# Building the first FFT's filter by casting loads instead of permutation matmuls, with stage A in four parts and products from ScalarE copies

## The chip, the cores and the metric

One core of one Trainium2 chip. The metric is the device time of one execution in microseconds (us). Most figures are medians of three to eleven executions. Each execution has a state, and all compared here are of the fast state (the single execution of before_look can't be given one). The rounds of experiments ran on different chips, so each ratio is against the kernel before in the same round. Traces are of one execution each. A trace's span is about 2 us less than the time of the same execution.

Engines are named as in the profile: PE is TensorE (PEld its weight loads), DVE is VectorE, ACT is ScalarE, POOL is GpSimd, SP is SyncE. "Granted clock" is the TensorE clock that was let through, 1.00 being full speed.

## The reference

```python
# batch 8, seq 3008, dim 256; then 24064 tokens, 256 -> 2048 -> 256
X = np.fft.rfft(x, axis=1)
F = (filt_r + 1j * filt_i)[None, :, :]
y = np.fft.irfft(X * F, n=x.shape[1], axis=1)
x = y.reshape(B * S, D)
h = np.maximum(x @ w_in, 0.0)
return (h * h @ w_out).astype(np.float32)
```

The FFT is made of matmuls with f16 constants. For one batch the stages are: A (x to u, written to DRAM and read back turned), B (u to the spectrum), products with the filter, P (products to ze), Z written to DRAM (dZ) and read back turned (zt), Y (zt to yt, the input of the feed-forward). For batch 0, stage A's result is turned on the chip and not through DRAM. Feed-forward then runs in 47 groups of 512 tokens, eight slots each, with the FFT stages of later batches laid into the slots.

## The kernel before

These are the parts that the change touches. The filter comes as float32 in dense rows; 0/1 matrices on PE put it in the order that the products need (psf), and ACT evicts it with the sign of the imaginary part:

```python
def place_f(im, k, *engs, rotate=False):
    ...
            nc.tensor.matmul(o, sPF[:, PQ.index((0, q)), :], f16s[0][:, im, a:a + d1 - d0],
                             start=True, stop=False)
            q, a = divmod(e1 + d0, QF) if c else (0, QF + d0)
            nc.tensor.matmul(o, sPF[:, PQ.index((1, q)), :], f16s[0][:, im, a:a + d1 - d0],
                             start=False, stop=True)
    ...
        if eng is nc.scalar:
            eng.activation(out=dst, in_=src, func=AF.Copy, scale=sign[:, 0:1] if im else 1.0)
```

Products are taken by DVE straight from PSUM; x of batch 1 and the weights come as float32 on SyncE's queue and are cast on the chip:

```python
    nc.vector.tensor_mul(
        out=prod,
        in0=ps.rearrange("p (a d) -> p a d", d=D).unsqueeze(1).to_broadcast([128, 2, 2, D]),
        in1=sF[:, :, 2 * p:2 * p + 2, :])

def load_wout(k):
    if k == 0:
        w32s[2] = p_h2.tile([128, NJT, 256], F32, tag="h2", name="wout32")
    c = slice(8 * k, 8 * k + 8)
    nc.sync.dma_start(out=w32s[2][:, c, :],
                      in_=moe_w_out.rearrange("(jt r) c -> r jt c", r=128)[:, c, :])
```

The prologue, cut to its order. While batch 0's Z travels through DRAM, 12 of the 16 units of batch 1's stage A are computed:

```python
for k in range(3):
    cast_wide(0, k, nc.vector, nc.gpsimd if k == 2 else nc.vector)
...                                  # constants, w_in, x of batch 1 (three loads of 1 MB)
for c in (0, 2, 1, 3):
    chunk_a0(c)                      # stage A of batch 0
...                                  # turn_u, first place_f
for k in range(7):
    if k < 6:
        unit_b(0, 2 * k)
        if k < 5:
            place_f(1, k + 1, nc.scalar)
        unit_b(0, 2 * k + 1)
    if k > 0:
        unit_p0(k - 1)
    if k < 4:
        place_f(0, k + 2, nc.scalar)
...
read_z(0, 0)
load_wout(0)
read_z(0, 1)
load_wout(1)
for c in (0, 2, 1):
    chunk_a(1, c)                    # stage A of batch 1, 12 of 16 units
for c in (0, 2, 1):
    write_u(1, c)
```

## Time and profile before

| | before |
|---|---|
| time, median of 3 (range) | 763.81 us (763.39 to 764.84) |
| span of the traced execution (time 765.42 us) | 763.6 us |
| stage A of batch 0 ends (last uT) | 17.75 us |
| last product of batch 0 ends | 40.55 us |
| first matmul of stage Y | 48.48 us |
| first feed-forward matmul (psH) | 49.93 us |
| first output matmul (psO) | 62.16 us |

The prediction below shows the main lines. Two more views are used later. First the DMA queues of the kernel before (packets, bytes, and the time that their packets took as a share of all 16 engines' span; q1 carries the loads of SyncE and ScalarE, q0 those of GpSimd):

```profile
q1 hardware_dynamic: 85704, 87.38, 37.1%
q0 software_dynamic: 19008, 20.43, 20.3%
```

q1 moved 87.38 MB in 0.371 x 763.6 = 283 us of full engine time, or 308 GB/s; q0 20.43 MB in 155 us, or 132 GB/s. The megabytes need care: a load that casts is counted by the f16 that it writes, and it reads twice that. The list of DMA issues shows it for w_out, here in the kernel before (float32) and in the changed kernel (cast), with the KB of each issue:

```profile
wout<-in_moe_w_out_dram SPq DMA_DIRECT2D x2, 1024.0 KB
...
sWout<-in_moe_w_out_dram POOLq DMA_DIRECT2D x2, 512.0 KB, 13.1
```

Of q0's bytes 9.4 MB are such loads of x (9184 KB in the list), the rest are the accumulating transfers of the products. Counted as read, q0 moved 29.8 MB, or 192 GB/s: a byte took 1.6 times as long as on q1, not more than twice.

Then two stretches of the busy time by stretch (length, then PE, weight load, DVE, ACT, POOL with their instructions, granted clock, DMA share, GB/s):

```profile
60.00:70.00 10.00, 9.29 (x65) 6.06 (x65) 7.16 (x10) 6.30 (x10) 0.00 (x0) 1.00 0.31 83
...
120.00:140.00 20.00, 19.91 (x246) 14.65 (x244) 17.36 (x21) 15.63 (x25) 0.00 (x0) 1.00 0.78 217
```

In the first group (60 to 70 us) DVE has room and the DMA engines are mostly idle; from 120 us on PE is saturated.

### The profile page before, as it was taken

To read this page: it belongs to the slowest core of one execution; us is meant where nothing else is said; L and a number is where in the kernel's file an instruction comes from. 1 tells how busy PE (TensorE), PEld (TensorE's weight loads), DVE (VectorE), ACT (ScalarE), POOL (GpSimd) and SP (SyncE) were. 2 spreads that over 40 slices of the span, in tenths; PEclk is the share of its full clock that TensorE was granted. 3 is DMA by queue.
4 is the path that set the end of the run, shared out by engine and by line. 5 is a ranking of instruction groups with operands and counts; after the bars stand their busy time and mean duration, and the time that the engine had idled before them with its cause. 6 is when DMAs were issued, how large, how long until landed. Compare 5 with 4: busy or idle time off the path is not lost.

```text
span 763.6 us, 19701 instructions
## 1 busy us (share of the span) xinstructions
PE 749.8 (98%) x8262; PEld 552.9 (72%) x8262; DVE 645.8 (85%) x714; ACT 578.8 (76%) x841; POOL 192.4 (25%) x260
## 2 busy tenths in 40 slices
PE   8988999999999999999999999999999999999998
PEld 5845766777777777877778777787777777777776
DVE  5857998899889888988979898798989989888783
ACT  3966777888877887788877877877877777777773
POOL 3800750244222321222312324033311222000000
PEclk9999999999999999999999999999999999999999
DMA  9985798765786467745585656775447334321011
GB/s 364 391 229 182 115 173 214 208 115 117 154 218 133 89 123 172 191 102 125 115 211 123 120 120 115 201 147 109 101 122 198 89 72 99 98 76 50 29 57 57
DMA packets 104946, 109.26 MB, mean 143 GB/s; under 512 B 9640, under 2 KB 93096, under 8 KB 102936
## 3 DMA queue, kind: packets, MB, share of 16 engines
q1 hardware_dynamic: 85704, 87.38, 37.1%
q0 software_dynamic: 19008, 20.43, 20.3%
q8 instruction: 65, 1.06, 0.6%
q14 instruction: 25, 0.20, 0.1%
q10 hardware_dynamic: 144, 0.18, 0.1%
HBM read 58.12 MB, written 48.23 MB: 139 GB/s over the span
## 4 chain that ended last, share of the span: by engine, by line
PE 88%; DVE 6%; DMA 3%; ACT 1%; issue 1%; POOL 0%; SPq 0%; ACTq 0%; DVEq 0%
PE psH L553 39%; PE psX L666 20%; PE psY L666 14%; PE psB L442 3%; PE psY L523 2%; PE psA L358 2%; PE psP L487 2%; DVE h L564 2%; PE psO L573 2%; DVE prod L450 1%; DMA ut<-dU 1%; PE warm L272 1%; DMA dU<-u 1%; PE psf L291 1%; PE psf L294 1%
## 5 line engine op out<-in xcount | busy, mean ns | idle before, releaser
L557 ACT ACTIVATE h<-psH 128x1024 f16<-128x1024 f32 x376 | 384.6, 1024 | 151.6 <-PE psH L553 147.4
L553 PE MATMUL psH<-yt,sWin 128*128 128x512 f16 (+7 forms) x1728 | 388.3, 352 | 1.4 <-DVE yt L532 0.6
L564 DVE TENSOR_TENSOR h<-h 128x2048 f16<-128x2048 f16 (+1 forms) x192 | 229.8, 1197 | 48.3 <-ACT h L557 48.0
L457 POOL DMA_DIRECT2D prod<-prod x168 | 138.6, 965 | 438.0 <-DVE prod L450 429.1
L553 PEld LDWEIGHTS <-sWin 128*128 128x128 f16 x1728 | 152.2, 98 | 99.4 <-issue 4.8
L666 PEld LDWEIGHTS <-sum 128*128 128x128 f16 x2880 | 177.5, 98 | 20.2 <-issue 0.2
L666 PEld LDWEIGHTS <-h 128*128 128x128 f16 x2160 | 133.6, 98 | 21.0
L450 DVE TENSOR_TENSOR prod<-psB,sF 128x1024 f16<-128x1024 f32 x84 | 102.4, 1219 | 16.4 <-PE psB L442 16.2
L666 PE MATMUL psX<-sT,sum 128*128 128x128 f16 x1440 | 102.5, 219 | 0.0
L666 PE MATMUL psY<-sT,sum 128*128 128x128 f16 x720 | 69.7, 219 | 0.0
L642 DVE TENSOR_TENSOR sum<-sum,h 128x2048 f16<-128x2048 f16 x45 | 55.0, 1222 | 1.0
L666 PE MATMUL psY<-sWout,h 128*128 128x128 f16 x720 | 55.0, 219 | 0.0
L666 PE MATMUL psX<-sT,h 128*128 128x128 f16 x720 | 54.9, 219 | 0.0
L666 PE MATMUL psY<-sWout,sum 128*128 128x128 f16 x720 | 54.7, 219 | 0.1
L645 DVE TENSOR_TENSOR sum<-h 128x2048 f16<-128x2048 f16 x45 | 54.8, 1217 | 0.0
L648 DVE TENSOR_TENSOR sum<-h,sum 128x2048 f16<-128x2048 f16 x45 | 54.7, 1217 | 0.0
L639 DVE TENSOR_TENSOR sum<-h 128x2048 f16<-128x2048 f16 x45 | 54.7, 1215 | 0.0
L362 ACT CAST u<-psA 96x512 f16<-96x512 f32 x90 | 52.2, 580 | 3.2 <-PE psA L358 2.8
L532 DVE CAST yt<-psY 128x376 f16<-128x376 f32 x62 | 33.7, 544 | 20.0 <-PE psY L523 19.9
L489 ACT CAST ze<-psP 128x512 f16<-128x512 f32 x84 | 48.9, 584 | 0.6 <-PE psP L487 0.4
L666 PE MATMUL psX<-sWout,h 128*128 128x128 f16 x720 | 47.6, 219 | 0.0
L523 PEld LDWEIGHTS <-zt 112*128 112x128 f16 x512 | 33.5, 98 | 18.5 <-issue 4.3
(86 smaller groups left out, 644.4 us busy)
## 6 DMA issues: line engine op xcount, KB each, us to landing
zt<-dZ SPq DMA_DIRECT2D x64, 192.0 KB
dU<-u SPq DMA_DIRECT2D x28, 384.0 KB
prod<-prod POOLq DMA_DIRECT2D x168, 64.0 KB, 2.7
dZ<-ze SPq DMA_DIRECT2D x28, 384.0 KB
x<-in_x_dram POOLq DMA_DIRECT2D x40, 192.0 KB, 5.0
ut<-dU SPq DMA_DIRECT2D x7, 1024.0 KB
xw<-in_x_dram SPq DMA_DIRECT2D x6, 1024.0 KB
out_dram<-top SPq DMA_DIRECT2D x31, 128.0 KB
```

The lines of the kernel that those rows point to most:

```text
L362: nc.scalar.copy(out=o, in_=pv)
L450: nc.vector.tensor_mul(out=prod, in0=ps.rearrange("p (a d) -> p a d", d=D).unsqueeze(1).to_broadcast([128, 2, 2, D]), in1=sF[:, :, 2 * p:2 ...
L457: nc.gpsimd.dma_start(out=prod[64 * i:64 * i + 64, 0], in_=prod[64 - 64 * i:128 - 64 * i, 1], accum_op=mybir.AluOpType.add)
L489: nc.scalar.copy(out=zes[(b, c)][:, 2 * i6:2 * i6 + 2, :], in_=ps.rearrange("p (a d) -> p a d", d=D))
L553: nc.tensor.matmul(ps[:, i, o:o + n], sWin[:, dt, jt * 128:(jt + 1) * 128], yts[b][:, dt, r:r + n], start=(dt == 0), stop=(dt == 1))
L557: nc.scalar.activation(out=h2[:, 2 * s:2 * s + 2, :], in_=ps, func=AF.Relu)
L564: nc.vector.tensor_mul(out=v, in0=v, in1=v)
L639: nc.vector.tensor_add(out=t, in0=a21, in1=a22)
L642: nc.vector.tensor_sub(out=t, in0=f[5], in1=a11)
L645: nc.vector.tensor_sub(out=t, in0=a11, in1=a21)
L648: nc.vector.tensor_sub(out=t, in0=a12, in1=f[6])
L666: nc.tensor.matmul(o[:, t, :], f[p][:, q, 128 * t:128 * t + 128], sg["w"][p][:, q, :], start=(m == 0 and p in (1, 2)), stop=(q == 7), skip ...
```

## The change

The intent was to shorten the prologue: no permutation matmuls and no evictions for the filter. GpSimd loads the filter with a cast to f16 into half rows (real parts on 64 partitions, imaginary on the other 64); a DVE copy swaps the halves (turn_f); signs are set later (settle_f). ACT copies stage B's result to f16 in SBUF so that the product runs from 16-bit SBUF operands. Stage A is split into four parts. Also, w_in, w_out and batch 1's x become casting loads of GpSimd, and all of batch 1's stage A moves from the wait for Z into the first feed-forward groups; idle matmuls, fill(22), take its place. The core of the diff:

```diff
-    def place_f(im, k, *engs, rotate=False):
-    ...
+    def load_f(c0, c1):
+        for im, filt in enumerate((filt_r, filt_i)):
+            v = filt[0:1504, :].rearrange("(j c) d -> j c d", c=47)
+            a, p = max(c0, 1), 64 * im
+            nc.gpsimd.dma_start(out=sF[p:p + 32, 0, c0:c1, :], in_=v[:, c0:c1, :])
+            nc.gpsimd.dma_start(out=sF[p + 32:p + 64, 0, a:c1, :], in_=v[:, 47 - a:47 - c1:-1, :])
+    ...
+    def turn_f(c0, c1):
+        for i in (0, 64):
+            nc.vector.tensor_copy(out=sF[i:i + 64, 1, c0:c1, :],
+                                  in_=sF[64 - i:128 - i, 0, c0:c1, :])
+    def settle_f(c0, c1):
+        nc.vector.tensor_scalar_mul(out=sF[64:128, 1, c0:c1, :], in0=sF[64:128, 0, c0:c1, :],
+                                    scalar1=-1.0)
+        nc.vector.tensor_copy(out=sF[64:128, 0, c0:c1, :], in_=sF[0:64, 0, c0:c1, :])
     ... (load_wout, cut)
-        nc.sync.dma_start(out=w32s[2][:, c, :],
+        nc.gpsimd.dma_start(out=sWout[:, c, :],
+    FC = ((0, 6), (6, 12), (12, 18), (18, 24))
+    HALVES = ((0, 0), (1, 0), (0, 1), (1, 1), (2, 0), (2, 1))
     ... (unit_b)
+        if b == 0:
+            ub = p_prod.tile([128, 2, D], F16, tag="prod", name=f"ub_{p}")
+            nc.scalar.copy(out=ub, in_=pv)
+            pv = ub
     ... (fft_plan)
-                for a in range(12, 16):
-                    fixed.append((2 + a / 2, unit_a, b, a))
-                moves.append((10.5, read_u, b))
+                for a in range(16):
+                    fixed.append(((3 if a < 8 else 4) + a / 2, unit_a, b, a))
+                for q in range(8):
+                    moves.append((1 + q, settle_f, 3 * q, 3 * q + 3))
+                moves.append((12.5, read_u, b))
-                r = 13.5 + 15 * p / 11 if b == 1 else ...
+                r = 16.5 + 13.5 * p / 11 if b == 1 else ...
     ... (prologue)
-    for c in (0, 2, 1, 3):
-        chunk_a0(c)
+    for n, cs in enumerate(((0, 2), (0, 2), (1, 3), (1, 3))):
+        for h in HALVES[n + 2:n + 3] if n > 1 else HALVES[2 * n:2 * n + 2]:
+            cast_wide(*h)
+        chunk_a0(n % 2, *cs)
     ...
-    for c in (0, 2, 1):
-        chunk_a(1, c)
+    load_rest()                      # rest of batch 1's x, and w_out, once Z has landed
+    fill(22)
```

## The prediction

> **What bounds the kernel now.** I read the page's busy line first, then the busy time by stretch, then the chain of waits up to the first feed-forward matmul, then the timeline of ScalarE (ACT), VectorE (DVE) and the DMA queues in that stretch. The page's first lines and the busy time by stretch:
>
> ```profile
> span 763.6 us, 19701 instructions
> PE 749.8 (98%) x8262; PEld 552.9 (72%) x8262; DVE 645.8 (85%) x714; ACT 578.8 (76%) x841; POOL 192.4 (25%) x260
> ...
> 20.00:30.00 10.00, 9.89 (x106) 8.71 (x104) 9.54 (x12) 9.46 (x11) 7.79 (x13) 1.00 1.05 411
> 30.00:40.00 10.00, 9.42 (x87) 7.88 (x85) 8.06 (x8) 9.21 (x10) 8.89 (x12) 1.00 0.82 308
> 40.00:50.00 10.00, 7.44 (x54) 4.60 (x53) 5.74 (x8) 6.10 (x10) 0.00 (x0) 0.98 0.74 213
> 50.00:60.00 10.00, 9.70 (x48) 4.26 (x48) 4.91 (x7) 7.47 (x10) 0.00 (x0) 0.85 1.09 305
> ...
> 200.00:400.00 200.00, 199.69 (x2249) 148.27 (x2248) 172.89 (x187) 160.20 (x238) 50.67 (x69) 1.00 0.65 149
> ```
>
> The columns of a stretch are its length and then PE, weight load, DVE, ACT, GpSimd (POOL), the granted clock, the DMA share and GB/s. After the start PE has no slack: 199.69 of 200 us. There a change counts by the PE work it adds or removes. The change keeps that part almost untouched; it rebuilds the prologue, in which batch 0 is transformed before any feed-forward matmul can start. What releases that start is in the chain of waits:
>
> ```profile
> 36.94 0.87 PE psP L473 x8
> 37.81 0.23 PE psB L442 x2
> 38.08 0.11 DVE prods L450
> 38.20 2.36 DVE prods L450 x2
> 40.60 0.61 PE psP L473 x4
> 41.24 1.02 ACT ze L475
> 42.27 2.35 DMA dZ<-ze
> 44.76 3.58 DMA zt<-dZ
> 48.34 0.14 issue
> ...
> 49.40 0.48 ACT yt L530
> 49.93 2.29 PE psH L553 x5
> ```
>
> Read it backwards. Feed-forward begins at 49.93. The last product of batch 0 ends at 40.56, so a tail of 9.4 us (last inverse matmuls, copy, write to DRAM, read back, first stage Y) is fixed. The question is when the last product ends. Before it, ACT is the bound: 9.46 and 9.21 of 10 us in 20 to 40, in strict turns of filter eviction (sF, real and imaginary) and ze:
>
> ```profile
> 28.99 1.02 ACT L302 ACTIVATE sF<-psf 128x1024 f16<-128x1024 f32 x1
> 30.09 1.11 ACT L302 ACTIVATE sF<-psf,sign 128x1024 f16<-128x1024 f32 x1
> 31.18 1.01 ACT L475 CAST ze<-psP 128x1024 f16<-128x1024 f32 x1
> ```
>
> DVE is second, with products at 1.22 us each. The start of the input DMA sets the rest: one MB of x lands each 2.5 us (casts at 6.20, 8.71, 11.21), so the queue delivers about 420 GB/s, and it is full until about 36 us.
>
> **What the Trainium skill says.** (1) "VectorE: DVE Perf Modes", section "The perf-mode tier table": a tensor-tensor operation runs at twice the rate with 16-bit operands in SBUF and at single rate with any PSUM operand; a 16-bit copy reaches four times. The trace agrees for the first: the product from PSUM of 1024 elements takes 1.22 us, a 1024-element f16 subtraction (sT) 0.68. No f16 copy on DVE is in this trace. (2) "DMA: Bandwidth & Descriptors", section "Issuing engines are not separate DMA queues": all queues share the same 16 engines. The trace agrees so far as one queue alone shows a share of 1.05 at 411 GB/s: a second queue has no spare capacity to find. (3) "SBUF — State Buffer", section "Who interferes with whom": two-port DVE modes shut out GpSimd's descriptor generation. Not shown in this trace. (4) "TensorE: Matmul & The Clock Gate", part 1: half the clock after an idle window of some 3.4 us. The trace agrees: 512-column matmuls are 0.43 us apart at the start and again from 49.93 (12 matmuls in 4.26 us, granted clock 0.85), 0.21 when warm.
>
> **The change, part by part.**
>
> Removed from the path up to the last product: the 108 permutation matmuls (PE is not the bound there); 13 sF evictions on ACT (6.6 + 5.1 + 1.1 = 12.8 us); one f cast on ACT (1.0) and one on DVE (0.7); GpSimd's casts. DMA is also lighter: 3 MB of x for batch 1 no longer come first.
>
> Products: 12 x (1.22 - 0.68) = 6.5 us less on DVE, for 12 ACT copies of 128x512 at 0.58 = 7.0 us. New on DVE: eight half-row copies (turn_f, 64 x 1536 f16). From (1), by the page's form (1536/4 + 150 cycles at 0.96 GHz), I estimate 0.56 us each, 4.4 us together.
>
> So after stage A the two engines have, worked out:
> ACT: 7 turned evictions x 0.60 + 12 copies x 0.58 + 5 ze x 1.02 + one half ze 0.58 = 4.2 + 7.0 + 5.1 + 0.6 = 16.9 us.
> DVE: 5 evictions x 0.68 + 12 products x 0.68 + turn_f 4.4 + half ze 0.7 = 3.4 + 8.2 + 4.4 + 0.7 = 16.7 us.
> They are balanced and coupled (each product waits for its ACT copy), so I allow 1 to 1.5 us of bubbles: 18 us.
>
> Where stage A ends. Half loads of 0.5 MB should land at 5.1, 6.3, 7.6, ... 11.3 us at 420 GB/s. But GpSimd begins the filter loads when the second half has landed, and they then take up to half of the engines. About 1.2 MB of x remain at 7.5 us; at 210 to 250 GB/s they end, with one us of completion, at 13.3 to 14.3. Cast 0.7, last 32 matmuls 1.4, eviction 0.6: last uT at about 16.2 (before: 17.75). So splitting stage A wins only 1.5 us. First turned matmuls 0.4, then 18 us: last product (and half ze) near 34.5. The tail is then about 9.0 (9.4 less 0.4 for the split ze): **feed-forward starts near 43, 7 us earlier.**
>
> The filter loads: 16 DMAs with cast, and two rows. A first x load from GpSimd in the steady part is issued in 0.51 us, one behind others in 1.15, and lands 5.0 us (median, 4.2 to 7.7) after issue. Four per chunk: last chunk issued between 16 and 26 us, landed by 22 to 31. It is needed at about 29, three units before the end. So it is just hidden in my reckoning.
>
> After the start. Added: stage A of batch 1 wholly inside the feed-forward, 16 single 512-column matmuls instead of 8: +8 x 0.215 = +1.7 us of PE; 6 more ACT copies (0.57) and 6 more DVE copies (0.69); settle_f, 16 f16 operations of 64 x 768 estimated at 0.36 (same form), 5.7 us of DVE, against 2.7 us of w_out casts removed. In slots 3 to 7 DVE then has about 0.6 (square) + 0.7 (settle) + 0.7 (stage A) + 0.3 (yt) = 2.3 us a slot, more than PE's 1.5. That makes the first group about 13 us, against 12.2 before. Saved: 22 filler matmuls keep the clock, so the 12 slow matmuls go at 0.21: -2.6 us. In the chain, batch 1's u goes out to DRAM and back and PE stands until it lands:
>
> ```profile
> 67.03 3.21 DMA dU<-u
> 70.26 3.83 DMA ut<-dU
> 74.14 0.39 PE psB L442 x2
> ```
>
> The wait counted for PE there is 1.3 us. The change puts the first stage-B unit five slots (some 10 us) after the last stage A, before it was three to four; the round trip is 7.1, so this wait should go: -1.3. Against it, 12 products are squeezed into 13.5 slots in place of 15, while DVE was busy all of 81.22 to 110.80 (14.38 of 14.38 and 15.08 of 15.20 us): I add 1 us. Sum after the start: +1.7 + 0.8 - 2.6 - 1.3 + 1 = -0.4, with the doubt on the plus side of DVE; some of the 2.6 was hidden behind ACT. I take -1 to +1, centre -0.5.
>
> **Total:** 763.8 - 7 - 0.5, rounded to **756 us**, 1.0% faster.
>
> **The rivals.**
> (a) The filter DMA becomes the bound: reversed rows are 192 pieces of 1 KB per DMA and GpSimd generates every one; DVE's casts and f16 copies may shut it out. For it: 16 issues at 1.15 us with landings up to 7.7 us, on engines that are already full. Against: 3 MB of x and the GpSimd casts are gone, and 0.51 us issues exist. The last chunk landing at 36 in place of 30 would bring the start to 48: about 761.
> (b) The early groups turn DVE-bound, or w_out and the second half of x for batch 1 come too late, since both wait for Z to land and go through GpSimd one after the other (w_out in 1 KB rows). For it: 2.3 us a slot against 1.5, and w_out is needed only about 13 us after the start. Each would cost 2 to 5 us: 758 to 761.
> (c) PE falls to the half clock in the prologue itself: it loses 108 matmuls and has only about 10 us of work in 18. Then 8-matmul steps take 1.7 us, fills 9.4 and the tail grows: 2 to 4 us back, 759.
> (d) Everything overlaps better than the old schedule: the last product at 30, the tail at 8.5, two more us from the removed waits. Start at 38.5: 750 to 751. To pass 2% (748.5) the start would have to come near 36, which balanced sums of 16.9 and 16.7 us after a stage A that ends at 16 do not allow, unless stage A ends by 14 with no bubbles.
> (e) The transfer is hidden anyway, and nothing moves: not likely, because the permutation's evictions stand on the chain (6.5% of the first 52 us as ACT sF alone, and 21.6% as PE psf).
>
> **Range and chances.** Start at 43 give or take 4, after-part give or take 2.5: 748.5 to 761.5, eight times in ten. Faster by over 2% needs (d) and more: 0.10. Slower by over 2% needs 779, a stall of over 20 us in a part where the old trace has none of that kind: 0.02. Within 2%: 0.88.
>
> **What would show it.** Right: last product near 34, first feed-forward matmul near 43; ACT and DVE both about nine tenths busy from 17 to 34; products in 0.68; no slow 512-column matmuls at the start; the stretch from 100 us after the start on is the same as before. Wrong in stage A: the second half of x lands well after 13.3 to 14.3. Wrong in (a): DVE waits for DMA before turn_f. Wrong in (b): PE idle before psO or psA with a DMA as releaser, or evictions of DVE as releaser in the first two groups. Wrong in (c): granted clock below 0.9 between 15 and 40. The prediction fails altogether if the tail of 9 us changes, since I took it over, or if the DMA rate of the filter loads is half of what I took.

## The result, and the profile after

The changed kernel took **773.54 us** (median of 4, 772.38 to 778.20) against 764.33 (763.39 to 765.91) for the kernel before on the same chip. The ratio is 1.013, with a 95% interval of 1.008 to 1.018. A ratio here is the mean time of one kernel's fast runs over that of the other's of the same rounds, so not quite the ratio of the medians. That is within 2%, but slower, and 12 us above the top of the predicted range. The traced execution is the slowest of the four (778.20 us; the others took 772.38 to 774.55), so its lags below are on the high side.

The first two lines of the page of the changed kernel:

```profile
span 776.2 us, 19474 instructions
PE 747.3 (96%) x8148; PEld 548.7 (71%) x8148; DVE 646.4 (83%) x734; ACT 572.0 (74%) x843; POOL 188.7 (24%) x262
```

PE is 2.5 us less busy over a span 12.6 us longer: the loss is waiting, not work. The busy time by stretch says where:

```profile
10.00:20.00 10.00, 5.05 (x71) 4.57 (x72) 5.48 (x10) 1.88 (x5) 6.27 (x11) 0.74 1.10 337
20.00:30.00 10.00, 7.66 (x73) 6.50 (x71) 6.22 (x11) 5.99 (x12) 5.41 (x11) 0.67 1.07 168
...
60.00:70.00 10.00, 6.98 (x44) 3.67 (x43) 9.58 (x18) 5.93 (x9) 0.00 (x0) 1.00 0.93 183
...
120.00:140.00 20.00, 17.41 (x172) 11.92 (x169) 14.30 (x17) 13.78 (x23) 3.02 (x6) 0.94 0.90 214
```

Against the rows of before, three places stand out. From 10 to 30 us no engine is near full and the granted clock is 0.74 and 0.67. From 60 to 70 us DVE is full (9.58) and PE is not. From 120 to 140 us PE loses 2.5 us and the clock falls again. And the DMA engines are full (1.07 in 20 to 30) at 168 GB/s, where before the same stretch moved 411 GB/s at 1.05 (part of this gap is the counting of casting loads). The queues of the whole run:

```profile
q1 hardware_dynamic: 82408, 77.80, 33.4%
q0 software_dynamic: 24544, 25.64, 24.3%
```

q1 carries 9.58 MB less and 24 us less of full engine time; q0 carries 5.21 MB more and 34 us more (0.243 x 776.2 - 0.203 x 763.6). The accumulating transfers of the products, which also run on q0, number 168 in both, so the difference is the new casting loads. Fewer bytes were counted, but about as many were read: the page's HBM line has 58.12 MB read before and 58.95 after, so the new casting loads read about 9.58 + 0.83 = 10.4 MB. For these the engines were busier by about 10 us of all sixteen: 34 us for 10.4 MB, where the float32 loads had 24 us for 9.58.

The chain of waits up to the first feed-forward matmul, in order of time, answers to the chain that the prediction shows for the kernel before:

```profile
9.92 1.02 DVE uT L356 x2
10.94 1.21 DVE xw L221 x2
...
17.79 1.02 DVE uT L356 x2
18.82 0.61 DVE xw L221
22.25 0.57 DVE uT L356
...
41.91 0.59 ACT ze L426
42.53 0.70 DVE ze L427
43.25 2.38 DMA dZ<-ze
45.76 3.37 DMA zt<-dZ
```

Where the old chain ran through ACT and products, the new one runs from 9.92 to 22.25 through DVE alone: evictions of stage A (uT), then casts of x (xw), then evictions again.

Stage times of all the traces (us). "3 to 4" is the stretch between two marks: a mark is the start of the first output copy (top<-psX) of a group of feed-forward, and the third and fourth are at 117 and 133 us in the kernel before. "Lag" is against the profile of before at the first of the 45 marks and at the last.

| trace | stage A end | last product | first psY | first psH | first psO | 3 to 4 | lag first, last |
|---|---|---|---|---|---|---|---|
| before | 17.75 | 40.55 | 48.48 | 49.93 | 62.16 | 16.6 | 0 |
| before_look | 16.32 | 40.21 | 48.09 | 49.53 | 61.74 | 16.6 | -0.5, -0.6 |
| after | 22.81 | 41.23 | 49.26 | 51.35 | 69.11 | 21.0 | 6.1, 12.5 |
| again | 23.33 | 41.89 | 49.84 | 51.82 | 68.62 | 20.5 | 5.6, 11.5 |
| e1_cast_ahead | 15.93 | 35.94 | 46.35 | 48.44 | 65.98 | 18.5 | 3.0, 7.7 |
| e2_filter_late | 22.22 | 39.73 | 48.14 | 49.59 | 65.68 | 18.4 | 2.7, 7.3 |
| e3_settle_in_wait | 22.72 | 41.08 | 48.88 | 50.97 | 66.42 | 18.3 | 4.1, 7.5 |
| e4_fill_long | 23.11 | 41.67 | 49.39 | 50.85 | 66.93 | 21.7 | 4.0, 11.2 |
| e6_no_copy | 23.21 | 47.94 | 56.33 | 57.79 | 73.93 | 20.3 | 10.9, 17.7 |
| e7_settle_psO | 23.02 | 40.11 | 47.86 | 49.31 | 62.70 | 18.4 | 0.3, 5.4 |
| e9_cast_ahead_fc3 | 15.80 | 36.33 | 44.03 | 45.49 | 62.93 | 21.8 | -0.1, 7.1 |
| e10_look_again | 22.58 | 39.73 | 48.94 | 50.40 | 68.03 | 16.6 | 6.4, 6.4 |
| c1_all_fc3 | 15.94 | 36.57 | 45.79 | 47.25 | 62.48 | 16.6 | -0.6, -0.1 |
| c2_all_fc4 | 16.00 | 36.54 | 47.45 | 48.90 | 62.56 | 16.6 | -0.4, 0.4 |
| c3_loads_moved | 16.62 | 35.05 | 45.17 | 47.26 | 59.83 | 17.4 | 1.0, 2.2 |
| c4_wout_as_before | 17.88 | 35.01 | 45.59 | 47.04 | 61.02 | 16.6 | -1.5, -1.0 |
| c5_and_fill26 | 16.70 | 35.61 | 46.11 | 47.56 | 60.19 | 16.6 | -2.7, -2.7 |
| c6_x_after_z | 15.78 | 35.93 | 44.32 | 45.77 | 59.50 | 16.6 | -2.7, -1.0 |

The changed kernel lies 6.1 us behind at the first mark, 7.3 at the third, 11.7 at the fourth, 12.7 at the seventh and 12.5 at the end: nearly all of the loss is made before about 145 us.

### The profile page after: what moved, and what is told of

Same layout as the page of the kernel before. It is cut to its first block, busy times and chain, and to the rows that moved or that the text cites.

```text
span 776.2 us, 19474 instructions
## 1 busy us (share of the span) xinstructions
PE 747.3 (96%) x8148; PEld 548.7 (71%) x8148; DVE 646.4 (83%) x734; ACT 572.0 (74%) x843; POOL 188.7 (24%) x262
## 3 DMA queue, kind: packets, MB, share of 16 engines
q8 instruction: 64, 1.05, 0.6%
HBM read 58.95 MB, written 48.23 MB: 138 GB/s over the span
## 4 chain that ended last, share of the span: by engine, by line
PE 84%; DVE 9%; DMA 3%; issue 1%; ACT 1%; POOL 0%; SPq 0%; ACTq 0%; DVEq 0%
PE psH L505 37%; PE psX L618 19%; PE psY L618 14%; PE psY L475 3%; PE psA L326 2%; PE psB L387 2%; DVE h L516 2%; PE psP L439 2%; DVE prod L400 2%; PE psO L525 2%; DMA zt<-dZ 1%; DMA prod<-prod 1%; DVE sum L591 1%; DMA dZ<-ze 1%; PE fill L310 1%
## 5 line engine op out<-in xcount | busy, mean ns | idle before, releaser
L330 ACT CAST u<-psA 96x512 f16<-96x512 f32 x96 | 55.6, 580 | 2.7 <-PE psA L326 2.3
L475 PE MATMUL psY<-sC,zt 112*128 112x94 f16 x512 | 43.6, 209 | 7.5 <-DMA zt<-dZ 5.1
```

The lines of the kernel that those rows point to most:

```text
L330: nc.scalar.copy(out=o, in_=pv)
L475: nc.tensor.matmul(ps[:, 94 * jj:94 * jj + 94], zt[:, 4 * (g % 2) + jj, dt * 128:(dt + 1) * 128], sSY, start=True, stop=True)
```

## The experiments

My theory was that three kinds of turns and waits cost the time: stage A's turns on DVE, the first group's DVE work and PSUM tiles, and batch 1's transform being later. The rivals were that loads arrive late, and that PE at half clock is the cause and not a consequence. All kernels gave correct results. Edits are against the changed kernel unless said otherwise.

**again.** No edit: the changed kernel's second profile.

> The changed kernel once more, unaltered, to see how much its stages vary between executions. Every theory expects the stages of the first profile within about 1 us: last eviction of stage A near 22.8, first feed-forward matmul near 51.4, first feed-forward-down matmul (psO) near 69.3, a lag behind the old kernel of 12 us after six groups, total 772 to 778 us. If the lag at the fourth group (4.4 us, PE waiting for Z of batch 1) is missing here, it is a matter of chance and not of the change.

Measured: 776.04 us (771.92 to 778.75), ratio 1.016 [1.012, 1.019], with the stage times above. The loss is real and sits in the same places. Its executions spread over 7 us, where those of the kernel before spread over 2.

**e1_cast_ahead.** Only the order of DVE's instructions in stage A is changed: the next part's casts come before the last part's evictions.

```diff
-        for h in HALVES[n + 2:n + 3] if n > 1 else HALVES[2 * n:2 * n + 2]:
+        for h in HALVES[n + 3:n + 4] if n else HALVES[0:4]:
```

> Only the order of VectorE's queue in stage A changes: the casts of the next part of x stand ahead of the evictions of the part before. Theory A (stage A became a chain of turns, PE waits for a cast, the cast waits behind evictions in VectorE's queue, the evictions wait for PE, with PE at half clock in the gaps): stage A's last eviction falls from 22.8 to 18 or less, the casts show waits for DMA or for nothing, and the start of feed-forward comes 3 to 5 us earlier; total 768 to 771. Rival B (the filter loads take DMA engines from x, so the later halves land late): the casts stand waiting for the DMA of x until about 14 and 18.5, stage A ends at 22 or later, and the time stays near 773.

Measured: stage A ends at 15.93 us, 6.9 earlier. DVE's timeline in this run (start, duration, engine, line, operation, tiles, shapes; in brackets the idle time before and its releaser):

```profile
8.59 0.69 DVE L221 CAST xw<-xw 128x1024 f16<-128x1024 f32 x1 [1.09 <-DMA xw<-in_x_dram]
9.91 0.69 DVE L221 CAST xw<-xw 128x1024 f16<-128x1024 f32 x1 [0.63 <-DMA xw<-in_x_dram]
10.52 1.02 DVE L356 CAST uT<-psA 128x384 f16<-128x384 f32 x2
```

Now the casts wait for the data (DMA), and they come at 8.59 and 9.91; in the changed kernel the same two began only at 10.86, behind evictions that waited for PE (2.12 us). DVE takes its instructions in the order in which they were written, so each part's data stood landed while DVE waited for the part before. The granted clock in 10 to 20 us rose from 0.74 to 1.00 at the same time: the half clock was a consequence of the gaps. But only 2.9 of the 6.9 us reach the first psH, and the total is 773.14 us (770.24 to 775.99), 1.012 [1.009, 1.016]: above the 768 to 771 that I expected, and not clear of the changed kernel's. DVE's waits from 14 to 45 us, and the chain of waits of the same run, name the rest:

```profile
DVE sF L248 <- DMA sF<-in_filt_i_dram: 3.0, 2, 2.5
```

```profile
37.96 5.02 DMA dZ<-ze
```

DVE now waits for the filter (3.0 us in two waits), and the last write of Z takes 5.02 us instead of 2.38, on DMA engines that are full (share 1.06 at 216 GB/s in 30 to 40 us).

**e2_filter_late.** The filter loads start only when the last half of x has landed.

```diff
-    nc.gpsimd.tensor_copy(out=tiny[:, 0:1], in_=xw32[1][0:1, 0, 0:1])
+    nc.gpsimd.tensor_copy(out=tiny[:, 0:1], in_=xw32[2][0:1, 4, 0:1])
```

> The filter loads of GpSimd wait for the last half of x instead of the second half. Rival B expects x to land earlier and stage A to end 3 us earlier or more (19 or less). Theory A expects stage A unchanged, 22 to 23, because nothing waits for x there; the filter then lands about 5 us later, near 25 to 31, so the products may start later, feed-forward at 51 to 55 and the total 773 to 777.

Measured: stage A ends at 22.22 us against 22.81 and 23.33; 774.73 us, 1.014 [1.012, 1.016]. Giving x the DMA engines for itself moves stage A by under 1.2 us, where a change of order alone moved it by 6.9. So late x was not what held stage A, though it was the one way in which the prediction had thought that stage A could go wrong.

**e3_settle_in_wait.** The 16 settle copies go from slots 1 to 8 into the wait for Z, where DVE is idle.

```diff
-                for q in range(8):
-                    moves.append((1 + q, settle_f, 3 * q, 3 * q + 3))
     ...
     fill(22)
+    for q in range(8):
+        settle_f(3 * q, 3 * q + 3)
```

> The sixteen settle operations of VectorE (5.7 us) move from slots 1 to 8 of the feed-forward into the wait for Z, where VectorE stands idle for some 7 us. Theory C (the first group became VectorE-bound through them and the stage A copies): the first group, from the first feed-forward matmul to the first psO, falls from 17.9 to 13 to 14 us, the total by 4 to 5 us, 768 to 770. Rival D (the first group is slow from the half clock and from late DMA of x and w_out): it stays at 17 or more and the time within 1 us of 773.

Measured: from the first psH to the first psO 15.45 us, against 17.76 and 16.80 (I had expected 13 to 14); 773.22 us, 1.013 [1.011, 1.014], where 768 to 770 was expected. The 16 copies took 0.35 us each, and about 2 us of them had been on the path. What remains in this group, from PE's waits in 50 to 75 us:

```profile
PE psA L326 <- ACT yt L482: 2.2, 3, 1.1
```

Stage A of batch 1 shares its two PSUM tiles with stage Y, and their evictions stand behind activations in ACT's queue.

**e7_settle_psO.** As e3, and stage A of batch 1 takes the PSUM tiles of the outputs, which are free in the first group.

```diff
-        ps = psF(f"psA_{b}_{a}")
+        ps = (psF(f"psA_{b}_{a}") if b > 1 or a > 7
+              else psO(f"psA_{b}_{a}").rearrange("p a d -> p (a d)"))
```

> On top of the settle operations moved into the wait (first group 15.45 us there): stage A of batch 1 in the first group takes PSUM tiles of the psO pool, which nothing uses before the second group, in place of the two psF tiles that it shares with stage Y. Theory (with settle gone, PE in the first group waits for psF tiles to be evacuated: a slot needs three of them from two buffers, and the evacuations stand behind the activations in ScalarE's queue): first group 13 us or less, total 2 to 3 us below the run with settle moved. Rival (the first group is bound by x arriving late or by ScalarE's own 11 us of work plus the half clock): 15 us or more, no gain.

Measured: the first group takes 13.39 us (e3 15.45), and the lag at the first mark is 0.3 us in place of 6.1. The total is 771.08 us (769.68 to 771.32), 1.009 [1.008, 1.011]: the lag grows again to 3.1 at the fourth mark and 5.4 at the end. The first group was worth 4.4 us against the first profile and 3.4 against the second, and its two halves are the settle copies and the PSUM tiles. About 2 us more of the smaller lag is an earlier start (first psH at 49.31 in place of 51.35), which this edit was not meant to move.

**e4_fill_long.** 33 idle matmuls in place of 22 in the wait for Z.

```diff
-    fill(22)
+    fill(33)
```

> 33 filler matmuls in place of 22 before the first stage Y, so that PE works until Z lands. Theory (the clock had halved again in the 2.5 us gap, so the first Y and the first eight 512-column matmuls go at half rate): from the first psY to the first feed-forward matmul 1.4 in place of 2.1 us, the eight matmuls 0.21 apart in place of 0.43, together 2 us less to the first psO; total 1.5 to 2.5 us below the unaltered kernel. Rival (ACT sets that pace anyway, and the fillers only delay Y): within 0.5 us.

Measured: from the first psY to the first psH 1.46 us in place of 2.09, and the granted clock in 50 to 60 us is 1.00 in place of 0.71, as the step of the half clock has it. One trace doesn't show that the longer fill did it: e2, e6, e7 and e9 take 1.45 or 1.46 us with 22 idle matmuls, so when the clock halves is in part chance. The total is 776.72 us, 1.017 [1.015, 1.018], no better than without this edit: of the 1.6 to 2.1 us won at the first mark 0.3 to 1.3 are left at the last, and the stretch 3 to 4 took 21.7 us here.

**e6_no_copy.** Products from PSUM again, without ACT's copy.

```diff
-        if b == 0:
+        if b < 0:
             ub = p_prod.tile([128, 2, D], F16, tag="prod", name=f"ub_{p}")
```

> Undoes one part of the change: the products of batch 0 read PSUM again, with no ScalarE copies. By the sums of the two engines after stage A (VectorE 16.7 + 6.5 = 23 us, ScalarE 10), the last product should come 5 to 6 us later than in the changed kernel, at 46 to 47, and feed-forward start at 56; total 778 to 780. If the chain between the engines and not their sums sets the pace, the shorter chain makes up for it: last product within 2 us of 41.2 and the time within 1 us of the changed kernel.

Measured: last product at 47.94 us in place of 41.23; 781.95 us (780.11 to 783.85), 1.024 [1.021, 1.027]. The groups of instructions of DVE in 20 to 50 us, with and without the copies:

```profile
L400 DVE TENSOR_TENSOR prods<-ub,sF 128x1024 f16<-128x1024 f16 x12 | 7.8, 686 | 1.0 <-ACT ub L398 0.6
```

```profile
L400 DVE TENSOR_TENSOR prods<-psB,sF 128x1024 f16<-128x1024 f32 x12 | 14.2, 1218 | 0.7 <-PE psB L387 0.3
```

The product takes 0.69 us from SBUF and 1.22 from PSUM, 6.4 us for the twelve, and nearly all of it shows at the last product (6.7) and in the total (6 to 8). This part of the change does what the prediction said of it.

**e9_cast_ahead_fc3.** As e1, with the filter in three pieces, so with four loads fewer.

```diff
-    FC = ((0, 6), (6, 12), (12, 18), (18, 24))
+    FC = ((0, 6), (6, 14), (14, 24))
```

> On top of the casts ahead: the filter in three pieces of 6, 8 and 10 columns in place of four of 6, so 14 loads in place of 18. In the run with casts ahead VectorE stood 2.5 us for the second piece of the filter, and GpSimd stood before its ninth load and later ones until earlier ones had landed. Theory (the filter is held up by the number of loads, each some 7 us from issue to landing with eight in flight): that wait falls below 1.5 us and the last product comes 1 to 2 us earlier than 35.9. Rival (the engines' time for 1 KB pieces is the limit, share 1.1): the wait stays or moves to the next piece, last product at 35.5 or later.

Measured: the last product comes at 36.33 us, no earlier than in e1, and DVE still waits 2.8 us for the filter (e1 3.0), so the rival holds there. But the first psH comes at 45.49 us, 4.4 us before the kernel before, and the write of Z in the chain of waits is short again:

```profile
38.36 2.36 DMA dZ<-ze
```

Yet the total is 772.78 us (767.16 to 775.63), 1.011 [1.007, 1.015]: the first group took 17.44 us, and the stretch 3 to 4 took 21.8.

**e10_plan_before and e10_look_again.** As e7, and four units of batch 1's stage A are done in the wait for Z, with the slots of batches 1 and 2 as in the kernel before (the diff is cut; reads of u and Z and the products' slots go back too).

```diff
-                for a in range(16):
-                    fixed.append(((3 if a < 8 else 4) + a / 2, unit_a, b, a))
+                for a in range(4, 16):
+                    fixed.append(((1 if a < 12 else 2) + a / 2, unit_a, b, a))
-                moves.append((12.5, read_u, b))
+                moves.append((10.5, read_u, b))
-                r = 16.5 + 13.5 * p / 11 if b == 1 else 9 + 25 * p / 11 if b == 2 else ...
+                r = 13.5 + 15 * p / 11 if b == 1 else 6 + 28 * p / 11 if b == 2 else ...
     ...
-    fill(22)
+    for a in range(4):
+        unit_a(1, a)
+    fill(28)
```

> Edit: e7 (settle copies in the wait for Z, PSUM tiles of psO) plus four of the sixteen stage A units of batch 1 done in the wait for Z, and the slots of batches 1 and 2 set back to those of the kernel before, so that batch 1's products end one slot earlier. Stage A of batch 0 is left as the change has it. My theory (the later slots of batch 1 are what costs 4 us before the seventh group's mark): the stretch from the third to the fourth mark of the seven-product copies falls from 18.4 us in e7 to about 16.6 (before: 16.6), TensorE waits there for no zt load of batch 1, and the total is 767 to 769 us (e7: 771.1). Rival (the wait is DMA contention, not the slot): the stretch stays at 18 us or more, TensorE still waits over 1 us for the zt load, total 770 to 772. A second rival: the extra units run on a half-speed TensorE in the wait for Z and push the first feed-forward matmul later than e7's 49.3 us; then the total stays too.

Measured: one execution in the slow state (1107.58 us at a granted clock of 0.652, left out of all comparisons) and three fast ones at 771.60, 771.67 and 777.27; 1.013 [1.010, 1.016]. The time missed the 767 to 769 that I expected of it, and the profile was of the slow execution and couldn't be read. So I ran the same kernel again:

> Edit: as in e10_plan_before, for a profile in the fast state. My theory: from the third to the fourth mark 16.6 us (e7 18.4, before 16.6) and no wait of TensorE for the zt load of batch 1; what then keeps the time at 771 us is earlier: a first feed-forward matmul at 50 us or later, or a first group of 15 us or more, from the x loads of batch 1 arriving late (TensorE waits for x 1 us or more in the first group). Rival: the stretch is 18 us again.

Measured: 773.64 us, 1.012 [1.011, 1.014]. The stretch 3 to 4 takes 16.6 us, as in the kernel before, against 18.4 in e7. In the changed kernel PE's waits of 95 to 145 us begin with

```profile
PE psY L475 <- DMA zt<-dZ: 2.6, 1, 2.6
```

and here that wait is gone; the lag is 6.4 us from the first mark to the last. The theory of the later slots holds. The second rival does too: the first psH comes at 50.40 us (e7 49.31), with the 28 idle matmuls ending 0.2 us before the first psY and no wait of PE for Z. And the first group now takes 17.63 us, and PE's waits of 40 to 68 us say why:

```profile
PE psA L326 <- DMA x<-in_x_dram: 4.4, 1, 4.4
```

The earlier units ask for x of batch 1 before GpSimd's load of it has landed.

**c1_all_fc3 and c2_all_fc4.** All three repairs together: e10 and e1, with the filter in three pieces (c1) or in four (c2).

> Edit: e10 plus the casts ahead of the evictions (e1) plus the filter in three pieces (e9). If the three causes add up (turns on VectorE in stage A, filter pieces and dZ writes late, batch 1's work moved onto the path): stage A ends near 15.9 us, first feed-forward matmul near 45.5 us (e9 45.49), first group at most 13.5 us (e7 13.39), third to fourth mark near 16.6 us; total 759 to 763 us, just under the kernel before (763.5). Rival (loads collide: an earlier start meets x, w_in and w_out still in flight, e9's first group was 17.4 us): the first group stays at 15 us or more and the total at 765 to 770 us.

> Edit: as the run before it, but with the filter in four pieces as the change has it. If the filter pieces cost what e9 against e1 showed (first feed-forward matmul at 45.49 against 48.44 us): it starts near 48 us and the total is 2 to 3 us above the three-piece version, 762 to 765 us. Rival (the late filter pieces are made up for by the later groups, as e9 and e1 had the same totals within their spread, 772.8 and 773.1): both within 1 us of one another.

Measured: c1 768.58 us (765.76 to 770.91), 1.007 [1.006, 1.009]; c2 766.30 us (765.30 to 770.10), 1.005 [1.003, 1.006]. Both are better than any before them, and both are above what I expected if the causes add up. The first psH comes at 47.25 and 48.90 us where about 45.5 and 48 were expected: as in e10, the 28 idle matmuls run until 0.2 us before the first psY and PE waits for no Z, so here they hold the start back themselves. In the traces c1 starts feed-forward 1.65 us earlier and loses it in the first group. (The medians have the reverse of the order that I expected, but the intervals touch, and c1's trace is of its fastest execution.) The chain of waits of c1 shows

```profile
46.97 15.21 DMA x<-in_x_dram
```

One load of x took 15.21 us to land, and PE waited 1.9 us for it. The first psO comes at 62.5 us in both.

**before_look.** The kernel before, for a second profile.

> Edit: none, the kernel before, for a second profile. Its profile on record has a span of 763.6 us, where the usual time of 763.4 us goes with a span near 761.4. If the profile on record was of a slower execution, this one ends near 761.4 us and shows where 2 us were lost, most likely at half clock in the wait for Z (granted clock 0.85 in 50 to 60 us). If not, the stage times are the same to 0.3 us.

Measured: 764.83 us, span 763.0, stage times within 0.5 us of the first profile apart from the end of stage A (1.4 us earlier). The half that expected a span near 761.4 failed, and the other half asked for 0.3 us, so the run decides little. The 11 timed executions of before in this round go from 763.18 to 766.24 us; those up to 763.93 have a granted clock of 0.999 or 1.000, the others 0.997 or 0.998. Both profiles, at 0.997 and 0.998, are of the longer kind. So traces that end at 763.6 and 764.2 us, as those of c1 and c2, don't mean the same median.

**c3_loads_moved.** c1 with four instead of two of the eight loads of batch 1's x (the texts call them halves) ahead of the wait for Z, the others before w_out, and fill(20).

```diff
-    for k in range(2):
+    for k in range(4):
         load_x(1, k)
     ... (load_rest)
-        for k in range(2, 6):
-            load_x(1, k)
-        for k in range(2):
-            load_wout(k)
-        for k in range(6, 8):
-            load_x(1, k)
+        for k in range(4, 8):
+            load_x(1, k)
+        for k in range(2):
+            load_wout(k)
```

> Edit: c1 with four instead of two halves of batch 1's x loaded ahead of the wait for Z, the other four before w_out, and 20 instead of 28 idle matmuls in the wait. If the loads are what stands in c1's way: no wait for x in the first group, first feed-forward matmul near 45.5 us (c1 47.25), first group at most 14 us, total 763 to 766 us (c1 768.6). Rival (the transfers as a whole are the bound between 40 and 65 us, their order is not): the wait moves to w_out or to Z (dZ write over 3 us), first output matmul still at 62 us or later, total 766 to 769 us.

Measured: 764.95 us (764.35 to 767.83), 1.001 [1.000, 1.002]. The wait for x is gone, the total is that of the first theory, and the rival is right too in what replaced it:

```profile
PE psO L523 <- DMA sWout<-in_moe_w_out_dram: 3.0, 1, 3.0
```

The next load in the line is now waited for. (This trace is of the slowest of the six executions, 767.83 us; the others took 764.35 to 765.46.)

**c4_wout_as_before and c5_and_fill26.** c4 is c3 with w_out as the kernel before loads it, in float32 on SyncE's queue behind the first reads of Z, with four casts on DVE; c5 is c4 with fill(26).

```diff
+            w32s[2] = p_h2.tile([128, NJT, 256], F32, tag="h2", name="wout32")
-        nc.gpsimd.dma_start(out=sWout[:, c, :],
+        nc.sync.dma_start(out=w32s[2][:, c, :],
     ...
+                for k in range(4):
+                    moves.append(((4.5, 5.5, 7.5, 7.5)[k], cast_wout, k, nc.vector))
     ...
-    fill(20)
+    fill(26)                         # c5 alone
```

> Edit: c3 with w_out loaded as the kernel before does it (float32 over SyncE's queue behind the first reads of Z, four casts on VectorE in the first group) instead of the casting load by GpSimd. If the casting load of 1 KB rows is what fills the DMA engines: no wait of TensorE for w_out (c3 3.0 us), first group under 12.6 us or at worst the same, total 761.5 to 763.5 us (c3 764.95, before 763.6). Rival (the bytes, not the form of the load, are the bound, or the four casts hold VectorE up): a wait for VectorE's yt or h2 squares takes its place, or for the zt reads, and the total is 764 to 767 us.

> Edit: c4 with 26 idle matmuls instead of 20 in the wait for Z. If TensorE's half clock after the wait costs (c3: 2.09 us from the first psY to the first feed-forward matmul, granted clock 0.83 in 40 to 50 us): that stretch takes 1.46 us, the total is 0.5 to 1 us under c4. Rival (as with e4_fill_long, what is won there is lost again at the next wait for a transfer): within 0.5 us of c4.

Measured: c4 763.94 us (762.36 to 765.60), 1.000 [0.999, 1.002]; c5 763.02 us (762.64 to 765.57), 1.000 [0.999, 1.001]. From 50 to 60 us, c3 and then c4:

```profile
50.00:60.00 10.00, 9.43 (x55) 4.64 (x55) 7.69 (x10) 9.36 (x14) 0.00 (x0) 1.00 1.32 215
```

```profile
50.00:60.00 10.00, 8.82 (x51) 4.21 (x50) 8.10 (x11) 9.28 (x13) 0.00 (x0) 0.99 1.09 276
```

With the float32 load the engines are less full (a share of 1.09 against 1.32; the GB/s don't compare, since c3's w_out counts half of what it reads), and the wait for w_out is gone. That casting is what cost the time isn't shown by it. c4 also issues w_out earlier, at 42.2 and 43.8 us against 45.0 and 45.9, and in another queue. And by the queue lines of the two runs the engine time for w_out changed little: 8.5 us cast (q0 186.9 to 178.4), 7.2 us in float32 (q1 262.0 to 269.2). PE waits 0.9 us for a yt of DVE (c3 0.4), which has the four casts to do; the 1 us of median gained on c3 lies inside the intervals. The start of c5 shows the longer fill no better than e4 did: it takes the expected 1.45 us from psY to psH, but so does c4 with 20 idle matmuls. 0.9 us of median against c4 lie inside the intervals too.

**c6_x_after_z.** c5 with two early loads of x and fill(20).

```diff
-    for k in range(4):
+    for k in range(2):
         load_x(1, k)
     ...
-    fill(26)
+    fill(20)
```

> Edit: c5 with two instead of four halves of batch 1's x loaded ahead of the wait for Z, and 20 instead of 26 idle matmuls, as the wait should be shorter. If the early x loads stand in the way of Z: last dZ write near 2.4 us (c5 4.49), first feed-forward matmul near 45.5 us (c5 47.56), no wait of TensorE for x over 0.5 us, and the total 1 to 2 us under c5, 761 to 762.5 us. Rival (the bytes have to go sometime): TensorE waits for x in the first group, 1 to 3 us, and the total is 762.5 to 764.5 us, as c5's.

Measured: the write of Z takes 3.13 us (c5 4.49, before 2.35), the first psH comes at 45.77, and the total is 764.05 us (762.61 to 766.57), 1.000 [0.999, 1.002]. The rival holds in the total, and not in its wait: PE's waits of the first group name no x. In the chain of waits it is w_out:

```profile
43.13 15.93 DMA wout<-in_moe_w_out_dram
```

This is a float32 load, and it too is long in landing (the two casting loads of c3 took 14.4 and 19.2 us).

So 1.8 us of an earlier start are paid back at a later landing: at the first mark c5 and c6 both lead by 2.7 us. From the 15th to the 16th mark c6 then loses 1.6 of its 2.7 us, which c5's trace does not. PE's waits of 296 to 318 us in c6 have one line:

```profile
PE psY L479 <- DMA zt<-dZ: 1.4, 1, 1.4
```

It is the wait for Z again, of a later batch, and c5's trace has no wait there. No version beats the kernel before; c5, with most of the causes found taken away, equals it.

## Why the prediction was wrong

It foresaw 756.0 us from a feed-forward start 7 us earlier and about nothing after it. The traced start came 1.4 us later, and what followed it took 11 us more. By its own steps:

- **"last uT at about 16.2" failed first: it was 22.8.** That step summed DMA landing, one cast, 32 matmuls and an eviction, as if only the last half's data mattered. It left out that the four parts take turns on DVE's in-order queue, with PE at half clock in the gaps (0.74 and 0.67, the sign that rival (c) named). e1 changed the order alone and ended stage A at 15.93 us; e2 shows that the cause named as the possible failure, late x, was not it. (A slip in the sum beside it: after 7.5 us three of the six half loads are to come, 1.6 MB and not 1.2. The right sum gives about 17.5 us or later for the end of stage A; e1 shows that this isn't what failed.)
- **"18 us" from there to the last product was right:** 18.4, against 18.3 by the prediction's numbers. Its terms were right too: 0.69 us a product, 0.55 for turn_f (0.56 estimated), 0.35 for settle_f (0.36). e6 measures the ACT copies at 6.4 to 6.7 us. That the whole came out right was in part luck: the late stage A gave the filter time to land. In e1, where stage A is in time, the same stretch takes 20.0 us, with 3.0 of waits for the filter.
- **"The tail is then about 9.0" failed: it was 10.1.** "Less 0.4 for the split ze" was wrong: the two halves came one after the other (ACT's 0.59, then DVE's 0.70, which waited 1.3 us for it), so the copy took 1.3 us in place of 1.0. And the idle matmuls ended 2.5 us before the first psY, which then ran at half clock up to the first psH (2.09 us against 1.45), as rival (c) says. In e4's trace this half clock is absent; it isn't worth anything in the total while the waits behind it stand.
- **"DMA is also lighter" was wrong as far as the engines' time goes.** The prediction counted bytes that come first, and not how long they take. The new casting loads took 34 us of full engine time for 10.4 MB read, the float32 loads that they replace 24 us for 9.58 MB. With the engines full, a repaired stage A gave only 2.9 of 6.9 us (e1: filter 3.0 us, write of Z 2.6 us longer), and c1, c2, c3 and c6 each trade one load's wait for another's. It is rival (a) in kind, which was put at "about 761", and the w_out half of rival (b). Which property of the new loads costs the time stays open: they cast, they go through another queue, and the filter and x come in shorter pieces than before. For w_out, in the same rows of 1 KB, casting made a difference of about 1 us (c3, c4). That this decides what is left of the gain once the turns are gone is argued: no run has all loads in float32.
- **"about 13 us" for the first group failed: 17.8 and 16.8.** Rival (b) was right in kind and DVE was full in 60 to 70 us. Two terms were missing: the settle copies could not overlap as taken (2 us, e3), and stage A's PSUM tiles are shared with stage Y (2 us, e7). Behind both is the fact that the kernel before did 12 of these 16 units in the wait for Z, where PE had nothing else to do. The prediction counted them as +1.7 us of PE; the place mattered more than the work.
- **"So this wait should go: -1.3" came true, and the sum of the part after the start failed all the same.** PE's wait for ut of batch 1 is gone in both traces of the changed kernel. "I add 1 us" for the squeezed products was right as well: the lag grows by 1.2 us from the first mark to the third. What has no term is the transfer behind them. Batch 1's products end 30.4 us after the first mark in place of 26.1, so its zt lands after PE needs it: PE waits 2.6 and 1.9 us for it, and from the third to the fourth mark it takes 20 to 22 us, or 18.3 to 18.5 in other runs with these slots, against 16.6. e10 with the old slots has 16.6 again. The five traces with 20 to 22 us have a half clock of 3.4 us at 131 to 145 us, the four with 18.3 to 18.5 have none. These two modes are what I see behind the 7 us spread of the changed kernel's executions; that they alone make it is argued from the traces, not shown.

Where the expected 7 us went can be read from c6: the first psH does come 4.2 us earlier and the last product 4.6, but the first psO only 2.7, and the total is unchanged. Part of it is lost to the loads and another part to the first group's DVE and ACT work, and 1.6 us in that trace to a Z wait at 312 us. c5's profile is 2.2 us shorter than the second one of before, with medians 0.7 us apart and ratio 1.000. Whether any of the early gain survives in most executions, or most of them lose it at a later wait as c6's trace did, stays open: it is below what these rounds can tell.

## What to carry to other kernels

Splitting a stage in parts makes gains only if each in-order queue holds the next part's first instruction ahead of the last part's last one; write the order of every engine down before believing in the sum of a single part. Before moving work out of a wait, ask what it cost there: hidden work that lands on the path costs its place, its buffers and the stage behind it. And count loads by engine time from the queue lines of the profile, not by bytes alone, and know what the bytes count (here a casting load shows what it writes): taking a cast away from the compute engines is not free when its load runs while the DMA engines are full.

## What the Trainium skill lacked or had wrong

- "DMA: Bandwidth & Descriptors", section "Anatomy of one DMA — SWDGE (gpsimd) path", gives 2.0 us and bytes over 436e3 for a load from GpSimd; for 1 MB of w_out in float32 that is an estimate of 4.4 us. Here w_out landed 12.4 and 13.8 us after issue and one load of x 15.2 (c1), in company with other loads. The page has no rate for casting loads among others: by the queue lines the new ones cost 34 us of full engine time for 10.4 MB read (about 310 GB/s), where float32 loads of 9.58 MB took 24 us (about 400 GB/s).
- "TensorE: Matmul & The Clock Gate", part 1, ties the half clock to idle windows of some 3.4 us; further down it tells of a kernel in which frequent short idles did it, and gives no figure for how much idling is enough. Here the clock fell to half at 14.75 us, after 6.83 us of full clock in which PE was busy 3.74, and the longest of PE's waits between 8 and 30 us was 1.7 us.
- Agreeing, for completeness: "VectorE: DVE Perf Modes" and its tier table. No f16 copy on DVE was in the old trace; the new ones, 0.55 us for 1536 elements and 0.35 for 768, bear out the four-fold rate to within 0.01 us of the estimate.
- No page that I used says what follows when work is split across a strictly ordered engine, a chain of turns, which was the largest single error here (6.9 us, e1).
